# A tuned decay-attention and expert kernel: the old state copied into the sum's bank in eight chunks, and the later chunks' order planned anew

## The chip, the cores and the metric

The kernel runs on one core of a Trainium2 chip. The metric is device microseconds of one execution. A profiled execution gives, beside its time, the span from its first to its last instruction and a trace of every engine.

## The reference

First comes a gated linear attention with a complex decay: for each of 4 batches and 8 heads a 48 x 48 state runs over 768 steps, and its output becomes the rows of a mixture of 8 experts with a fixed capacity. Cut to what matters:

```python
for t in range(S):                       # per batch b and head h
    new_re = ar * S_re - ai * S_im       # ar, ai: a_re, a_im scaled so that the size is at most 0.999
    new_im = ar * S_im + ai * S_re
    S_re, S_im = new_re + k_t v_t^T, new_im
    y[t] = q_t @ S_re
x = y laid out as 3072 tokens of 384 numbers
logits = x @ w_gate                      # 8 experts, each takes 384 tokens, the best pairs first
out[tokens of e] = relu(x[tokens of e] @ w1[e]) @ w2[e]
```

## The kernel before, in words

**Staging.** The 768 steps of a batch are six chunks of 128, so there are 24 chunks, numbered 0 to 23 through all four batches; cc is the chunk's place in its batch. Three chunks make a group (`GROUPS`), eight groups in all. The elementwise work on the decay (square, Ln, Exp, Arctan, Sin on ScalarE, products and running sums on VectorE; stages F1 to F11, S, G1 to G5, A1 to A2, N0, N2, T1 to T3 in `elementwise`) is done per group, and is the bulk of VectorE's and ScalarE's work. T1 and T3 write the sines and cosines `CS`.

**A chunk, stage by stage** (`turns` and `unit`):

- RQ (VectorE): `f <- kq, CS`, the rotation of keys and queries. K (SyncE's DMA queue): six transfers `KQ <- f` stack it for TensorE.
- SC (TensorE): `sc <- KQ`, scores, in two halves. MK (VectorE): `am <- sc, mask`, two halves.
- FL (TensorE): `kp <- ident, KQ`, keys turned, only for cc below 5. KC (ScalarE): `kt <- kp`.
- ST (TensorE): `U <- V, kt`, eight products that are the chunk's part of the state. CA (TensorE): `U <- W, ident`, one product of 384 columns with a unit matrix that adds the old state W to the sum in the same bank. WM (VectorE): `W <- U, KQ`, the sum times the gate is the state for the next chunk. W and its successor lie in two tiles in turn.
- MX (TensorE): `y <- am, V` and `y <- KQ, W`. XC (ScalarE): `xT <- y`. FN (TensorE): `xp <- pick, xT`. XE (ScalarE): `x <- xp`. LR (VectorE): `lg <- xp`, the logits. XS: the store of `x`.
- FI (TensorE): `sc <- mask, f`, products whose result nobody reads, so many for each chunk as the table `FILL` says, three pieces a chunk. They stand ahead of the chunk's scores.

**Two ways to the sum.** Where a chunk is in `SEEDED` (line 691: 20, 21 and 22 before), CA is left out. Instead US (ScalarE, after the WM of the chunk before) copies W into the bank, and ST adds its eight products onto it without a start flag:

```python
U = mine["U"] = sums.pop(i) if i in SEEDED else ps.tile([96, 384], F32, name="U")
...
sums[i + 1] = ps.tile([96, 384], F32, name="U")
nc.scalar.activation(sums[i + 1], W[(cc + 1) % 2][:, :384], AF.Copy)
```

**What sets the order.** `attention` records every step with a cost, its inputs and a number `prio` (the chunk, with a little added or taken off), and then `OFF` adds an offset by the step's kind. `in_order` is a planner: it lets a model of the engines run, and on each engine the ready step with the smallest number goes first. The order it finds is then fixed by dependences (`Queue.follow`), engine by engine, so on the chip each engine works through its list strictly in that order. A step's kind carries ">" where its number is at least `LATE` (99 before, so none does). After the attention the same lists go on with the routing and the experts, which a second planner orders.

Of the kernel before, what the change touches and what calls it, by code (L numbers as in the profile page):

```python
# [21 lines left out]
B, H, S, D = 4, 8, 768, 48  # L22
# [234 lines left out]
def attention(nc, real, tc, z, kq_in, a_re, a_im, v_tok, xd, later):  # L257
# [28 lines left out]
    def op(key, eng, cost, prio, fn, deps=()):  # L286
        kind = key[0][0] if type(key[0]) is tuple else key[0]
        o = Op(eng, cost, fn, [made.get(d) for d in deps], prio)
        o.kind = kind + ("<" if prio < EARLY else ">" if prio >= LATE else "")
        ops.append(o)  # L290
        made[key] = o
        if o.kind.rstrip("<>") in ("lk", "lv"):
            moved(o, 128, (24 if key[0] == "lk" else 12) * T)
        return o
# [161 lines left out]
    def turns(i):  # L456
# [10 lines left out]

        f_free = [("K", i - F_BUFS), ("FI", i - F_BUFS, len(FILL.get(i - F_BUFS, ())) - 1)] if i >= F_BUFS else []
        op(("P0", i), "pool", 0.75, i, lambda: g.tensor_copy(
# [21 lines left out]
    def unit(i):  # L491
# [11 lines left out]
        def keep(n):  # L503
            if ("sc", 0) not in mine:
                mine["sc", 0] = ps.tile([128, 4, 128], F32, name="sc", bufs=2)
            for _ in range(n):
                nc.tensor.matmul(mine["sc", 0].rearrange("p h t -> p (h t)"), tiles["f", i][:, 0, 0, 128:256].bitcast(BF)[:, 1::2],
                                 z.mask.bitcast(BF)[:, None].to_broadcast([128, 2, 256]), start=True, stop=True)
        parts = FILL.get(i, ())
        for n, x in enumerate(parts):  # L510
# [17 lines left out]
        if cc < 5:  # L528
# [14 lines left out]
            def state():  # L543
                U = mine["U"] = sums.pop(i) if i in SEEDED else ps.tile([96, 384], F32, name="U")
                for h in range(8):
                    nc.tensor.matmul(U[:, h * 48:h * 48 + 48], mine["kt"][:, h], v_[:, c * 384 + h * 48:c * 384 + h * 48 + 48],
                                     start=(h == 0 and i not in SEEDED), stop=(h == 7 and (not cc or i in SEEDED)),
                                     skip_group_check=True)
# [4 lines left out]
            op(("ST", i), "pe", 1.33, at - 0.2, state, [("KC", i, 0), ("KC", i, 1), ("lv", gi), ("WM", i - 1), ("WM", i - 2), ("US", i)])  # L553
            if cc and i not in SEEDED:
                op(("CA", i), "pe", 0.65, at - 0.1, carry, [("ST", i), ("WM", i - 1), ("WM", i - 2)])
# [12 lines left out]
            def seed():  # L568
                sums[i + 1] = ps.tile([96, 384], F32, name="U")
                nc.scalar.activation(sums[i + 1], W[(cc + 1) % 2][:, :384], AF.Copy)  # L570
            if i + 1 in SEEDED:
                op(("US", i + 1), "act", 0.371, at + 0.3, seed, [("WM", i)])
# [78 lines left out]
    for o in ops:  # L651
        o.prio += OFF.get(o.kind, 0.0)
    for o in in_order(ops, STEP, HOP, DMA_WAIT, DMA_DONE, START, SLACK):
# [30 lines left out]
DMA_DONE = 1.1  # L684
LATER = [2.4, 4.6, 0.9, 3.6]
START = dict(pe=0.0, act=0.3, dve=2.6, pool=4.3, dma=0.65)
OFF = {"US": 0.0, "A1": 10.399, "A2": -9.822, "BE": 0.131, "CA": -2.118, "F1": -1.107, "F10": 3.443, "F11": 7.184, "F2": -0.925, "F3": 5.421, "F4": 5.223, "F5": -4.22, "F6": 3.011, "F7": -5.852, "F8": -2.715, "F9": -5.359, "FI": 6.816, "FI<": 9.377, "FL": 9.859, "FL<": -5.873, "FN": 12.915, "G1": 1.011, "G2": -1.21, "G3": -11.062, "G4": -0.449, "G5": -6.433, "K": -5.895, "KC": -14.0, "LR": -0.075, "MK": -7.142, "MX": 7.176, "N0": 3.163, "N2": 4.716, "P0": 12.184, "RQ": 2.776, "S": 7.92, "SC": 10.153, "SC<": -1.898, "ST": 11.563, "ST<": -6.332, "T1": 8.558, "T2": 10.974, "T3": -7.584, "TL": -6.667, "WM": -3.298, "XC": -9.548, "XC<": -8.705, "XE": 10.454, "XS": 9.28, "la": -9.643, "la<": -6.574, "later": 0.869, "li": -8.149, "li<": -7.975, "lk": -3.51, "lv": -2.528, "table": -8.414}
CHAIN = ("scalar", "vector", "tensor", "gpsimd", "sync")
F_BUFS, KC_BUFS = 4, 5
FILL = {0: (6, 6, 6), 1: (2, 2, 2), 2: (4, 4, 4), 3: (2, 2, 2), 5: (6, 6, 6), 7: (4, 4, 4), 8: (1, 1, 1), 9: (3, 3, 3), 10: (1, 1, 1), 11: (3, 3, 3), 12: (3, 3, 3), 13: (2, 2, 2)}  # L690
SQ = ()
SEEDED = (20, 21, 22)
EARLY, LATE = 0, 99


class Router:
# [828 lines left out]
```

## Time and profile before

| | us |
|---|---|
| median of 3 runs (lowest to highest) | 488.49 (487.59 to 489.42) |
| the profiled execution, its own time | 489.1 |
| its span, first to last instruction | 487.3 |
| TensorE busy in the span | 430.0 (88%) |
| VectorE busy | 400.8 (82%) |
| ScalarE busy | 309.5 (64%) |

The attention takes the first 222 us of the span and the routing and the experts the rest. The time of an execution is some 2 us more than its span. The tables count an engine as busy while one of its instructions runs; TensorE's ends are modelled.

### The profile page before, as it was taken

Reading aid. Unit: us, or ns where it says so; the run is one execution under the profiler, and the core shown is the slowest. Engines: PE = TensorE matmul, PEld = TensorE weight load, DVE = VectorE, ACT = ScalarE, POOL = GpSimd, SP = SyncE. Lnnn points to the kernel's source line nnn. Section 1 sums busy time; section 2 is a strip of 40 time slices with the busy share of each in tenths; the row PEclk is TensorE's granted clock in tenths of the full one; section 3 lists DMA queues with packets and bytes.
Section 4 is the critical chain, followed back from the end, with each engine's and each line's share of the span. In section 5 each row is a group of like instructions: output and inputs, shape, how many; then the busy total and the mean of one; then the engine's idle time right before and its main releaser. Section 6 shows DMA issues by size and latency. Waiting matters only on the chain.

```text
span 487.3 us, 9823 instructions
## 1 busy us (share of the span) xinstructions
PE 430.0 (88%) x3626; PEld 386.5 (79%) x3626; DVE 400.8 (82%) x1023; ACT 309.5 (64%) x585; POOL 123.6 (25%) x218
## 2 busy tenths in 40 slices
PE   0019999999999999995489899999999999999996
PEld 0006887889789999984378799999989899999995
DVE  6999999999999999845869889998888899434250
ACT  7999988999899849721056448375562837443341
POOL 7321020303031411132031233240503236040202
PEclk9999999999999999996589999999999999999999
DMA  7807886878896855521252526280714438430001
GB/s 259 323 5 205 274 263 201 271 218 271 226 304 196 266 153 160 164 82 67 101 207 98 211 78 228 85 324 18 298 43 179 179 104 342 171 98 0 34 16 50
DMA packets 33104, 82.52 MB, mean 169 GB/s; under 512 B 4352, under 2 KB 23552, under 8 KB 29984
## 3 DMA queue, kind: packets, MB, share of 16 engines
q1 hardware_dynamic: 25632, 41.96, 27.6%
q0 software_dynamic: 6848, 38.95, 21.7%
q10 hardware_dynamic: 576, 0.98, 0.5%
q8 instruction: 29, 0.48, 0.4%
q14 instruction: 19, 0.16, 0.1%
HBM read 53.49 MB, written 9.44 MB: 129 GB/s over the span
## 4 chain that ended last, share of the span: by engine, by line
PE 71%; issue 11%; ACT 7%; DVE 6%; DMA 2%; POOL 1%; SPq 1%; POOLq 1%; ACTq 0%; DVEq 0%
PE acc L136 30%; PE sc L136 14%; PE y L136 8%; PE U L136 7%; PE xp L136 4%; PE kp L136 3%; PE cnt L136 3%; ACT s L136 3%; DVE ind L136 1%; DMA ai<-in_a_im 1%; POOL out L136 1%; ACT L278 1%; PE thr L136 1%; ACT w1h L136 1%; ACT p L136 1%
## 5 line engine op out<-in xcount | busy, mean ns | idle before, releaser
L136 PE MATMUL acc<-w2h,hh 128*128 128x384 f32 x192 | 62.5, 345 | 0.2 <-DVE hl L136 0.2
L136 PE MATMUL acc<-w2h,hl 128*128 128x384 f32 x192 | 62.1, 344 | 0.0
L136 PE MATMUL acc<-w2l,hh 128*128 128x384 f32 x192 | 61.9, 344 | 0.2 <-DVE w2l L136 0.2
L136 PE MATMUL acc<-xl,w1h 128*128 128x384 f32 x192 | 61.2, 343 | 0.1
L136 PE MATMUL acc<-xh,w1l 128*128 128x384 f32 x192 | 61.1, 342 | 0.0
L136 PE MATMUL acc<-xh,w1h 128*128 128x384 f32 x192 | 60.0, 338 | 0.0
L136 PE MATMUL sc<-mask,f 128*128 128x512 bf16 x111 | 28.7, 405 | 35.0 <-DVE f L136 35.0
L136 ACT ACTIVATE hh<-acc 128x384 fp32r<-128x384 f32 x64 | 30.7, 491 | 38.9 <-PE acc L136 37.2
L136 POOL DMA_INDIRECT out<-ot,idx x24 | 25.3, 1055 | 107.7 <-ACT ot L136 102.5
L136 DVE SCALAR_TENSOR_TENSOR hl<-acc,hh 128x384 fp32r<-128x384 f32 x64 | 34.6, 551 | 21.3 <-ACT hh L136 20.6
L136 PEld LDWEIGHTS <-f 128*128 128x128 bf16 x111 | 10.6, 103 | 48.1 <-DVE f L136 35.0
L136 PE MATMUL sc<-KQ 96*128 96x128 f32 x384 | 48.1, 277 | 0.7 <-DMA KQ<-f 0.7
L136 PEld LDWEIGHTS sc<-KQ 96*128 96x128 f32 x384 | 45.1, 192 | 1.5 <-issue 1.4
L136 ACT ACTIVATE parts<-cnt 32x8 f32<-32x8 f32 x120 | 20.2, 168 | 39.9 <-PE cnt L136 37.7
L136 DVE TENSOR_TENSOR f<-kq,CS 128x1536 f32<-128x1536 f32 x24 | 41.6, 1749 | 1.5 <-ACT CS L136 1.0
L136 DVE TENSOR_TENSOR ind<-m,thr 128x768 bf16<-128x768 f32 (+1 forms) x45 | 33.8, 769 | 3.9 <-PE thr L136 2.3
L136 PE MATMUL y<-am,V 128*64 128x128 f32 x384 | 36.5, 278 | 0.0
L136 PEld LDWEIGHTS acc<-w2h,hh 128*128 128x128 f32 x192 | 35.6, 189 | 0.6 <-DVE hl L136 0.6
L136 PEld LDWEIGHTS acc<-w2l,hh 128*128 128x128 f32 x192 | 35.6, 188 | 0.4 <-DVE w2l L136 0.3
L136 POOL DMA_DIRECT2D xd<-x x22 | 13.4, 608 | 88.8 <-ACT x L136 88.5
L136 DVE TENSOR_TENSOR am<-sc,mask 128x512 f32<-128x512 f32 x48 | 31.7, 680 | 5.0 <-PE sc L136 4.8
L136 PEld LDWEIGHTS acc<-w2h,hl 128*128 128x128 f32 x192 | 35.8, 188 | 0.0
(204 smaller groups left out, 1107.9 us busy)
## 6 DMA issues: line engine op xcount, KB each, us to landing
KQ<-f SPq DMA_DIRECT2D x144, 128.5 KB, 2.7
kq<-in_kq SPq DMA_DIRECT2D x8, 1152.0 KB, 7.0
V<-in_v SPq DMA_DIRECT2D x8, 576.0 KB, 5.3
xd<-x POOLq DMA_DIRECT2D x22, 192.0 KB
ar<-in_a_re SPq DMA_DIRECT2D x6, 576.0 KB, 5.1
ai<-in_a_im SPq DMA_DIRECT2D x6, 576.0 KB, 6.2
ar<-in_a_re SPq DMA_DIRECT2D x2, 384.0 KB, 4.2
ar<-in_a_re SPq DMA_DIRECT2D x2, 192.0 KB, 3.9
```

The costliest lines, as they stand in the source:

```text
L136: r = f(*a, **k)
L278: real.scalar.add_instruction(ins)
```

## The change

The three seeded chunks become eight: every chunk of the last two batches that has an old state and a sum (13 to 16 and 19 to 22). For 13, 14, 15, 16 and 19 the copy US is new and the product CA goes. `LATE` is 11.5, so that all steps of the chunks from 12 on get offsets of their own (kinds with ">"), and `FILL` loses its entries for chunks 10 (3 products) and 11 (9) and gains 14 (18) and 18 (12). Of the offsets two stand here for the table.

```diff
-OFF = {"US": 0.0, ..., "F11": 7.184, ...}
+OFF = {..., "F11": 7.184, "F11>": -0.841, ..., "US>": 2.849, ...}
...
-FILL = {0: (6, 6, 6), 1: (2, 2, 2), 2: (4, 4, 4), 3: (2, 2, 2), 5: (6, 6, 6), 7: (4, 4, 4), 8: (1, 1, 1), 9: (3, 3, 3), 10: (1, 1, 1), 11: (3, 3, 3), 12: (3, 3, 3), 13: (2, 2, 2)}
+FILL = {0: (6, 6, 6), 1: (2, 2, 2), 2: (4, 4, 4), 3: (2, 2, 2), 5: (6, 6, 6), 7: (4, 4, 4), 8: (1, 1, 1), 9: (3, 3, 3), 12: (3, 3, 3), 13: (2, 2, 2), 14: (6, 6, 6), 18: (4, 4, 4)}
 SQ = ()
-SEEDED = (20, 21, 22)
-EARLY, LATE = 0, 99
+SEEDED = tuple(range(13, 17)) + tuple(range(19, 23))
+EARLY, LATE = 0, 11.5
```

The order of steps moves on every engine from about 80 us of the span to the attention's end. The routing and the experts keep theirs. Three places follow.

TensorE at the end of the attention, before: `KQ_122` is the stack of chunk 21, `KQ_123` of 22, `KQ_124` of 23. The rows left out are the products `y`.

```order
L136 MATMUL kp<-ident,KQ_122 128x96 x8
L136 MATMUL sc<-KQ_122 128x128 x8
L136 MATMUL U<-V_115,kt 96x48 x8
...
L136 MATMUL kp<-ident,KQ_123 128x96 x8
L136 MATMUL sc<-KQ_123 128x128 x8
L136 MATMUL U<-V_115,kt 96x48 x8
...
L136 MATMUL sc<-KQ_124 128x128 x8
L136 MATMUL xp<-pick,xT 128x112 x8
```

The same stretch in the changed kernel:

```order
L136 MATMUL kp<-ident,KQ_122 128x96 x8
L136 MATMUL sc<-KQ_122 128x128 x8
L136 MATMUL U<-V_113,kt 96x48 x8
L136 MATMUL kp<-ident,KQ_123 128x96 x8
L136 MATMUL sc<-KQ_123 128x128 x8
...
L136 MATMUL U<-V_115,kt 96x48 x8
L136 MATMUL xp<-pick,xT 128x112 x4
...
L136 MATMUL sc<-KQ_124 128x128 x8
L136 MATMUL U<-V_115,kt 96x48 x8
L136 MATMUL xp<-pick,xT 128x112 x4
```

The state products `U` of chunk 20 now stand behind the scores of 21, those of 21 behind the products `y` of chunk 21, and those of 22 behind the scores of 23. The turned outputs `xp` go one by one.

VectorE around the rotation of chunk 21 (`f_118`), before; `ext` is the reduction over the first eighteen chunks' logits.

```order
L136 TENSOR_TENSOR p<-p,s_1615 128x3x128
L136 TENSOR_TENSOR W_109<-U,KQ_125 96x384
L136 SCALAR_TENSOR_TENSOR zi<-zi,s_1624 128x128 x3
L136 TENSOR_TENSOR f_118<-kq,CS 128x6x256
L136 TENSOR_TENSOR am<-sc,mask 128x512 x2
L136 TENSOR_TENSOR f_119<-kq,CS 128x6x256
L136 TENSOR_TENSOR kq<-kq,s_1624 128x3x128
L136 TENSOR_TENSOR kq<-kq,zi 128x3x128
L136 TENSOR_TENSOR W_111<-U,KQ_121 96x384
L136 TENSOR_REDUCE lg_89<-xp 128x16
L136 TENSOR_REDUCE ext<-lg_89 128x2
L136 COPY lg_89<-ext 128x16
```

The same place in the changed kernel:

```order
L136 SCALAR_TENSOR_TENSOR p<-ar,ai 128x3x128
L136 TENSOR_TENSOR am<-sc,mask 128x512
L136 TENSOR_TENSOR p<-p,s_1651 128x3x128
L136 TENSOR_REDUCE lg_89<-xp 128x16
L136 TENSOR_REDUCE ext<-lg_89 128x2
L136 COPY lg_89<-ext 128x16
L136 TENSOR_TENSOR f_118<-kq,CS 128x6x256
L136 TENSOR_TENSOR f_119<-kq,CS 128x6x256
```

One logits reduction, `ext` and its copy have moved ahead of the rotation of chunk 21, and the `W` of chunk 19 (`KQ_125`) has moved behind it. Farther ahead, out of these rows, the step `p <- p, s` (128x3x256) of this group now stands ahead of the rotations of chunks 18 to 20, where it stood behind them.

ScalarE around the sines of chunks 15 to 17 in the changed kernel, where the first of the new copies stands:

```order
L278 ACT_TABLE_LOAD
L136 ACTIVATE xT<-y 128x512
L136 ACTIVATE kt<-kp 128x384 x2
L136 ACTIVATE CS<-neg 128x3x384
L136 ACTIVATE xT<-y 128x512
L136 ACTIVATE U<-W_111 96x384
L136 ACTIVATE x<-xp 128x384 x2
L136 ACTIVATE CS<-p,cb 128x3x384
```

Before, nothing but one `x` stood between the two rows `CS` of this group, and the cosine row came first; the copy `U <- W_111` (for chunk 13) and the outputs of the chunks before are now ahead of the second.

## Rows read from the trace of the kernel before

**Rows 1.** Busy us by stretch: length, PE, PEld, DVE, ACT, POOL; PEclk, DMA share, GB/s.

```profile
127.00:151.00 24.00, 24.00 (x247) 21.07 (x248) 23.40 (x35) 21.52 (x28) 5.27 (x7) 1.00 0.86 264
151.00:175.00 24.00, 24.00 (x277) 21.75 (x275) 23.88 (x40) 19.52 (x27) 6.51 (x8) 1.00 0.67 207
175.00:195.00 20.00, 19.84 (x221) 18.26 (x220) 19.18 (x34) 16.16 (x27) 3.29 (x6) 1.00 0.66 180
...
211.00:223.00 12.00, 10.39 (x121) 9.52 (x120) 3.42 (x10) 3.01 (x6) 2.66 (x14) 1.00 0.27 84
```

**Rows 2.** The chain that ended last, 181 to 220 us: start, us, what.

```profile
181.40 0.66 PE kp L136 x8
...
195.58 0.88 PE xp L136 x8
...
201.71 0.66 PE kp L136 x8
202.37 1.81 PE sc L136 x16
204.19 1.32 PE U L136 x16
...
211.32 2.45 DMA KQ<-f
...
217.93 1.91 PE y L136 x32
```

**Rows 3.** VectorE in order of time, 179 to 208 us: start, us, instruction, idle before.

```profile
179.16 0.95 DVE L136 TENSOR_TENSOR p<-p,s 128x768 f32<-128x768 f32 x1
180.03 0.55 DVE L136 TENSOR_SCALAR neg<-ar 128x384 f32<-128x384 f32 x1
...
193.62 1.76 DVE L136 TENSOR_TENSOR f<-kq,CS 128x1536 f32<-128x1536 f32 x1 [0.43 <-issue]
195.30 1.28 DVE L136 TENSOR_TENSOR am<-sc,mask 128x512 f32<-128x512 f32 x2
...
199.10 0.55 DVE L136 TENSOR_TENSOR W<-U,KQ 96x384 f32<-96x384 f32 x1
200.22 0.23 DVE L136 TENSOR_REDUCE lg<-xp 128x16 f32<-128x64 f32 x1 [0.58 <-ACT x L136]
200.49 0.45 DVE L136 TENSOR_REDUCE ext<-lg 128x2 f32<-128x288 f32 x1
200.97 0.18 DVE L136 COPY lg<-ext 128x16 f32<-128x16 f32 x1
...
206.31 1.76 DVE L136 TENSOR_TENSOR f<-kq,CS 128x1536 f32<-128x1536 f32 x1 [0.53 <-ACT CS L136]
```

**Rows 4.** VectorE at the rotations of chunks 12, 15 and 18, and three scans.

```profile
124.19 3.42 DVE L136 TENSOR_TENSOR f<-kq,CS 128x1536 f32<-128x1536 f32 x2
...
137.38 1.04 DVE L136 TENSOR_TENSOR_SCAN zi<-zi,s 128x128 f32<-128x128 f32 x3
...
148.91 1.75 DVE L136 TENSOR_TENSOR f<-kq,CS 128x1536 f32<-128x1536 f32 x1
...
172.65 1.75 DVE L136 TENSOR_TENSOR f<-kq,CS 128x1536 f32<-128x1536 f32 x1
```

**Rows 5.** The chain earlier: nine filling products, and U with the carry.

```profile
106.81 2.05 PE sc L136 x9
...
189.04 2.01 PE U L136 x18
```

**Rows 6.** TensorE in order of time: the turned keys of chunk 12.

```profile
134.81 0.82 PE L136 MATMUL kp<-ident,KQ 96*128 96x96 f32 x8
```

**Rows 7.** ScalarE in order of time: sines, turned keys, and two of the three copies U.

```profile
147.37 1.16 ACT L136 ACTIVATE CS<-neg 128x1152 f32<-128x1152 int32 x1
148.42 0.87 ACT L136 ACTIVATE kt<-kp 128x384 f32<-128x384 f32 x2
149.16 0.61 ACT L136 ACTIVATE xT<-y 128x512 f32<-128x512 f32 x1
...
193.44 0.47 ACT L136 ACTIVATE U<-W 96x384 f32<-96x384 f32 x1
...
208.56 0.49 ACT L136 ACTIVATE U<-W 96x384 f32<-96x384 f32 x1 [1.98 <-DVE W L136]
```

More of the change, by code (lines that the diff above doesn't have):

```diff
@@ L686 @@
 START = dict(pe=0.0, act=0.3, dve=2.6, pool=4.3, dma=0.65)
-OFF = {"US": 0.0, "A1": 10.399, "A2": -9.822, "BE": 0.131, "CA": -2.118, "F1": -1.107, "F10": 3.443, "F11": 7.184, "F2": -0.925, "F3": 5.421, "F4": 5.223, "F5": -4.22, "F6": 3.011, "F7": -5.852, "F8": -2.715, "F9": -5.359, "FI": 6.816, "FI<": 9.377, "FL": 9.859, "FL<": -5.873, "FN": 12.915, "G1": 1.011, "G2": -1.21, "G3": -11.062, "G4": -0.449, "G5": -6.433, "K": -5.895, "KC": -14.0, "LR": -0.075, "MK": -7.142, "MX": 7.176, "N0": 3.163, "N2": 4.716, "P0": 12.184, "RQ": 2.776, "S": 7.92, "SC": 10.153, "SC<": -1.898, "ST": 11.563, "ST<": -6.332, "T1": 8.558, "T2": 10.974, "T3": -7.584, "TL": -6.667, "WM": -3.298, "XC": -9.548, "XC<": -8.705, "XE": 10.454, "XS": 9.28, "la": -9.643, "la<": -6.574, "later": 0.869, "li": -8.149, "li<": -7.975, "lk": -3.51, "lv": -2.528, "table": -8.414}
+OFF = {"A1": 10.399, "A1>": 12.582, "A2": -9.822, "A2>": -7.131, "BE>": 0.184, "CA": -2.118, "F1": -1.107, "F10": 3.443, "F10>": -2.977, "F11": 7.184, "F11>": -0.841, "F1>": 9.456, "F2": -0.925, "F2>": -4.698, "F3": 5.421, "F3>": 14.0, "F4": 5.223, "F4>": 10.113, "F5": -4.22, "F5>": -2.47, "F6": 3.011, "F6>": -1.065, "F7": -5.852, "F7>": 10.7, "F8": -2.715, "F8>": 0.086, "F9": -5.359, "F9>": 12.455, "FI": 6.816, "FI<": 9.377, "FI>": 4.422, "FL": 9.859, "FL<": -5.873, "FL>": -1.602, "FN": 12.915, "FN>": 6.34, "G1": 1.011, "G1>": -8.004, "G2": -1.21, "G2>": 3.76, "G3": -11.062, "G3>": -4.808, "G4": -0.449, "G4>": 2.176, "G5": -6.433, "G5>": -0.588, "K": -5.895, "K>": 2.748, "KC": -14.0, "KC>": -0.932, "LR": -0.075, "LR>": 5.74, "MK": -7.142, "MK>": -13.968, "MX": 7.176, "MX>": -8.176, "N0": 3.163, "N0>": 1.825, "N2": 4.716, "N2>": 9.631, "P0": 12.184, "P0>": -12.123, "RQ": 2.776, "RQ>": -10.775, "S": 7.92, "S>": 6.55, "SC": 10.153, "SC<": -1.898, "SC>": 0.655, "ST": 11.563, "ST<": -6.332, "ST>": 1.524, "T1": 8.558, "T1>": 2.908, "T2": 10.974, "T2>": -0.665, "T3": -7.584, "T3>": 7.342, "TL": -6.667, "TL>": 4.19, "US>": 2.849, "WM": -3.298, "WM>": 3.698, "XC": -9.548, "XC<": -8.705, "XC>": -5.369, "XE": 10.454, "XE>": -1.616, "XS": 9.28, "XS>": 8.325, "la": -9.643, "la<": -6.574, "la>": 2.746, "later>": -9.256, "li": -8.149, "li<": -7.975, "li>": 3.861, "lk": -3.51, "lk>": 4.282, "lv": -2.528, "lv>": -9.512, "table": -8.414}
```

## The prediction

> **What bounds the kernel now.** I read the busy times by stretch first, then the chain that ended last, then VectorE's and ScalarE's lists in order of time. The change lies in the attention, so only that is costed. In the stretches from 127 to 195 us TensorE is busy all but 0.16 us and VectorE all but 1.5 of 68 us, while ScalarE has 2.5, 4.5 and 3.8 us free [rows 1]. Two engines are full, and the chain shows how they meet: VectorE makes a rotation, the queue stacks it, and TensorE takes it up. The last rotation ends at 206.31 + 1.76 = 208.07 us [rows 3] and its last transfer lands at 211.32 + 2.45 = 213.77 [rows 2], so a stack is there 5.7 us after its rotation. TensorE's last long run begins with the turned keys of chunk 21 at 201.71 and ends with the products y of chunk 23 at 217.93 + 1.91 = 219.84 [rows 2]. The rotation of chunk 21 ends at 195.3 [rows 3], so its stack lands at 201.0, and TensorE comes 0.7 late to it. The attention's end is therefore set by the rotation of chunk 21 plus TensorE's work behind it, as long as TensorE reaches it in time.
>
> **The change part by part.**
>
> Carries: U with the carry takes 2.01 us [rows 5] and without it 1.32 [rows 2], so 0.69 each. Five go: 3.45 us off TensorE.
>
> Fills: nine take 2.05 us [rows 5], 0.228 each. Twelve go at chunks 10 and 11 (2.7), thirty come at 14 and 18 (6.8). TensorE's work as a whole grows by 4.1 - 3.45 = 0.65 us.
>
> Copies: five at 0.48 us [rows 7], 2.4 on ScalarE. Their cover is the free time of ScalarE above. Without it they would delay the sines, and with them the rotations (a rival below).
>
> Moved steps on VectorE, counted from the two orders up to each group's first rotation. Chunk 12: three scans and one logits reduction more, 1.04 + 0.23 [rows 3, 4], some 1.2. Chunk 15: six scans and two reductions more, some 2.4. Chunk 18: p, neg, one mask half and one reduction more, 0.95 + 0.55 + 0.64 + 0.23, less their overlaps, about 2.0 [rows 3]. Chunk 21: a reduction, ext and its copy more, the W of chunk 19 less, 0.23 + 0.45 + 0.18 - 0.55 = 0.3 [rows 3]. So the middle groups' stacks come later and chunk 21's nearly at the old time. The first three are hidden if TensorE is no earlier than the stacks: chunk 12's now lands at 125.9 + 1.2 + 5.7 = 132.8 [rows 4], chunk 18's at 172.65 + 1.75 + 2.0 + 5.7 = 182.1 [rows 4].
>
> Is TensorE in time for chunk 21? It began the turned keys of chunk 12 at 134.81 [rows 6]. Now 2.7 of fills are gone ahead of that, and one xp (0.88 [rows 2]) has come: 133.0, just behind the stack. From there to the keys of chunk 18 it took 181.40 - 134.8 = 46.6 us [rows 2, 6]. Now 6.8 of fills come, four carries (2.8) and one xp (0.9) go: 49.7, so 182.7, behind that stack by 0.6. From the keys of 18 to those of 21 the new order has three kp, three sc, two U, two and a half y and three xp: 2.0 + 5.4 + 2.6 + 4.8 + 2.6 = 17.4 [rows 2], with 0.3 for the seams 17.7, so 200.4.
>
> The stack of chunk 21: VectorE waits 0.43 ahead of that rotation [rows 3], for the cosines. The step p that starts ScalarE's work for them now stands ahead of three rotations (over 5 us), so I let that wait go. 0.3 more work, 0.4 less wait: the stack lands at 200.9, and TensorE begins there with 0.5 in hand.
>
> The last run: the new order has two kp, three sc, three U, three y and two xp up to the end of chunk 23's y, 1.3 + 5.4 + 4.0 + 5.7 + 1.8 = 18.2 [rows 2]. The old one has one U less, 16.9, and took 18.13; the other 1.2 is mostly the wait for chunk 23's stack. That stack comes earlier now, since VectorE's W of chunk 20 stands behind the last rotation (0.55 [rows 3]), and the scores of 23 are asked for only 12.3 us into the run, at 213.2. So that wait goes, and the moved U takes its place: with seams 18.5, end at 219.4. What follows (xp, x, the logits) is as before.
>
> The sum: 219.4 against 219.84, **0.4 us less**. Against the profiled execution's own 489.1 that is 488.7. That execution lies 0.6 above the median of the runs, so against 488.49 I forecast 488.1. The bounds of the unknown part are VectorE's waits: if all 0.8 us that it was free from 175 to 195 [rows 1] goes, 0.4 more is won; if none goes, 0.4 is lost.
>
> **The rivals.**
>
> TensorE comes late (ends slower). The fills taken out at chunks 10 and 11 may be followed by waits of the same size, and then the thirty new ones are pure work. If TensorE still reaches chunk 12 at the old time plus the xp, it comes 2.7 later everywhere, 2.2 of it behind the 0.5 in hand: 488.1 + 2.2 = 490.3. Waits for masks or the W that now stand behind other steps add to that in full; two of 0.5 (the W is 0.55 long [rows 3]) make 491.3. For it: TensorE has no free time in this stretch [rows 1], and the sum grows by 0.65. Against it: by the counts above it is behind the stacks at 12 and 18 by 0.2 and 0.6 only, so real work fills the gap. It decides from 0.5 us of such waits on. Chance 0.23, half of it above 490.9.
>
> ScalarE's queue. A copy that waits for its W holds everything behind it: one copy stood 1.98 us so [rows 7]. Around the sines of chunk 15 the new order has two kt, one xT, two x and one copy more ahead of the second table of sines, 0.87 + 0.6 + 1.0 + 0.5 = 3.0, the x taken like a copy [rows 7], and the old slack is 148.91 - 148.53 = 0.4 [rows 4, 7]. VectorE's own 2.4 covers nearly all. At chunk 21, where 0.3 is the cover, all five copies (2.4) ahead of the sines would cost up to 2.1: 490.2. Against it stand 4.5 and 3.8 us free on ScalarE [rows 1]. Chance 0.12. The Trainium skill (PSUM — Partial Sum Buffer, Engine vs sequencer instructions) states the rule behind this rival: ScalarE's and VectorE's queues are strictly first in, first out. The waiting copy in the rows agrees.
>
> The clock. With gaps where fills stood, the granted clock could fall to 1.2 GHz. It was 1.00 from 211 to 223 us with TensorE busy 10.39 of 12 [rows 1], so gaps of a fraction of a microsecond do nothing. If a stretch with 5 us of work ran at half, 5 us would come on top, 0.5 of it in hand: 492.6. Chance 0.04. The Trainium skill (TensorE: Matmul & The Clock Gate, Part 1) says that the low clock is the default and that only sustained activity lifts it, which speaks against taking fills out; by that rule alone the time would come out at this rival's.
>
> More is won than I see. If chunk 21's rotation came 2.2 us earlier, TensorE being there too, 485.9. VectorE is busy all but 0.8 us in that stretch [rows 1] and has not less to do, which speaks against it. Chance 0.07.
>
> **How the numbers follow.** The forecast has 0.54. Differences within 0.5% (2.4 us, about what a measurement of this kernel can tell from none) run from 486.05 to 490.9. The forecast, ScalarE's rival and half of the late TensorE lie between them, 0.54 + 0.12 + 0.11 = 0.77; for terms that I left out I move 0.07 of that to faster and 0.04 to slower, which leaves 0.66. Slower is the other 0.12 of the late TensorE, the clock's 0.04 and that 0.04: 0.2. Faster is 0.07 + 0.07 = 0.14. The range goes from the forecast with all waits gone (487.7) less the 0.9 by which the runs lie under their median, 486.8, to the late TensorE with its masks, 491.3.
>
> **What would show it.** TensorE's U with unit matrix: 16 instructions, not 26; copies U: 8; fills: 129. The rotation of chunk 21 within 0.5 of 193.5; the keys of 21 at about 200.9, the end of chunk 23's y near 219.4, and no wait for chunk 23's stack. I am wrong if TensorE shows waits over 0.5 us between 105 and 182 or reaches chunk 18 after 183.2, if VectorE waits longer for CS, if the granted clock falls under 1.00 ahead of 220, or if the attention's end moves by over 2.4 us either way.

## The result, and the profile after

The changed kernel takes 493.03 us (median of 6 runs, 490.62 to 498.08) against 487.77 for the kernel before (6 runs, 487.44 to 489.42): a ratio of 1.0108, 95% interval 1.008 to 1.0135. It is 1.1% slower, and the forecast of no difference (488.1, range 486.8 to 491.3) was wrong. A second set of six gave 1.0121 (1.0089 to 1.0153). A ratio leaves out runs that lie over 1.5% above the fastest of their kernel (here the one of 498.08). The changed kernel's runs lie 7.5 us apart, in the second set 4.9, those of the kernel before 2.0.

The profiled run took 493.2 with a span of 491.4. The first two lines below are stretches from the start of rotation 9: to the start of rotation 18, and to the end of the last y. The others are around chunk 13. The columns are those of [rows 1].

```profile
101.27:180.40 79.13, 76.00 (x770) 65.86 (x770) 73.89 (x111) 67.37 (x87) 12.81 (x22) 0.98 0.70 216
101.27:226.70 125.43, 121.40 (x1293) 107.72 (x1291) 108.79 (x173) 96.59 (x137) 21.82 (x40) 0.99 0.64 191
...
140.00:142.00 2.00, 0.54 (x7) 0.57 (x8) 2.00 (x7) 0.70 (x1) 0.00 (x0) 1.00 0.89 220
142.00:144.00 2.00, 2.00 (x9) 0.87 (x8) 1.39 (x3) 1.98 (x4) 0.00 (x0) 0.50 1.03 275
144.00:146.00 2.00, 2.00 (x11) 1.62 (x10) 1.92 (x2) 2.00 (x3) 1.83 (x2) 0.64 0.92 378
```

The same two stretches of the kernel before:

```profile
100.49:172.65 72.16, 72.16 (x748) 62.74 (x748) 71.26 (x106) 65.53 (x82) 16.76 (x21) 1.00 0.77 238
100.49:219.84 119.35, 118.53 (x1285) 106.21 (x1283) 108.74 (x173) 94.14 (x132) 26.70 (x40) 1.00 0.67 202
```

To the last y the new kernel needs 6.1 us more. By TensorE's column that is 2.9 us more busy time and 3.2 more idle; some 1.7 of the busy time are the low clock around chunk 13, since a second profile without it (below) has 119.7 us busy. By VectorE's column, up to rotation 18 it has 2.6 us more work (73.89 - 71.26) and is idle 5.24 us where it was idle 0.90. Of the 5.24 only 1.3 lie ahead of TensorE's wait at chunk 13 (141.46, below) and 4.0 behind it, so this column alone does not tell which engine begins the loss.

VectorE in order of time (start, us, instruction, idle before it and what ended that), with the rotations that answer to [rows 3, 4]:

```profile
112.89 0.69 DVE L136 TENSOR_TENSOR am<-sc,mask 128x512 f32<-128x512 f32 x1 [0.75 <-PE sc L136]
...
127.31 5.07 DVE L136 TENSOR_TENSOR f<-kq,CS 128x1536 f32<-128x1536 f32 x3
...
144.08 1.36 DVE L136 TENSOR_TENSOR kq<-kq,s 128x1152 f32<-128x1152 f32 x1 [0.69 <-ACT s L136]
...
147.92 0.69 DVE L136 TENSOR_TENSOR am<-sc,mask 128x512 f32<-128x512 f32 x1 [1.22 <-PE y L136]
...
150.73 0.23 DVE L136 TENSOR_REDUCE lg<-xp 128x16 f32<-128x64 f32 x1 [1.23 <-PE xp L136]
...
156.17 5.07 DVE L136 TENSOR_TENSOR f<-kq,CS 128x1536 f32<-128x1536 f32 x3
...
180.40 5.09 DVE L136 TENSOR_TENSOR f<-kq,CS 128x1536 f32<-128x1536 f32 x3
...
198.46 3.42 DVE L136 TENSOR_TENSOR f<-kq,CS 128x1536 f32<-128x1536 f32 x2
...
210.26 1.75 DVE L136 TENSOR_TENSOR f<-kq,CS 128x1536 f32<-128x1536 f32 x1
```

Rotation 12 begins 3.1 us later than before (0.8 of it is there before the orders part: the first step in which VectorE's two lists differ begins at 83.64 us, where it began at 82.78), 15 by 7.3, 18 by 7.8, 21 by 4.8, 23 by 4.0. TensorE's keys kp, which answer to [rows 2, 6], and six fills (the second line):

```profile
141.46 1.00 PE L136 MATMUL kp<-ident,KQ 96*128 96x96 f32 x8 [1.89 <-DMA KQ<-f]
142.26 2.76 PE L136 MATMUL sc<-mask,f 128*128 128x512 bf16 x6
...
188.61 0.88 PE L136 MATMUL kp<-ident,KQ 96*128 96x96 f32 x8
...
206.95 0.85 PE L136 MATMUL kp<-ident,KQ 96*128 96x96 f32 x8 [0.18 <-DMA KQ<-f]
...
211.62 0.85 PE L136 MATMUL kp<-ident,KQ 96*128 96x96 f32 x8 [0.69 <-DMA KQ<-f]
```

At chunk 13 TensorE waits 1.89 us for the second stack of its group, and then the granted clock is 0.50 and 0.64: the six fills take 2.76 us (1.46 in the second profile, where the clock is 1.00). Chunk 18 comes at 188.61, 7.2 us later than in [rows 2], and from there to the last y's end (226.70) it is 38.1 us, about as before (219.84 - 181.40 = 38.4).

That second stack is late for two reasons. Rotation 12 begins 2.3 us later than before, counted from rotation 9, and the stack's last transfers are slow. The first line below is from 132.9 to 134.3 us, the other two are from 135.5 to 136.3 (the number of issues, the size of one and the median us from issue to landing; `xd <- x` is the store of x):

```profile
KQ<-f SPq DMA_DIRECT2D x3, 128.5 KB, 2.5
...
xd<-x POOLq DMA_DIRECT2D x2, 192.0 KB, 4.5
KQ<-f SPq DMA_DIRECT2D x2, 128.5 KB, 5.0
```

In the kernel before, one store stood there and the last transfer of chunk 13 took 3.7 us; here it took 5.2, and the 1.5 between them are most of the wait. At chunk 16 the last two took 5.1 and 5.0 us, again with two stores issued meanwhile, and 2.4 and 2.5 before. In the new order x of two chunks is often evicted and stored together. No run moved the stores alone, so their part is seen in the traces and not tested.

Behind the attention this profile is 2.8 us shorter than before (264.7 against 267.5 from the last y to the end of the span). The kernels below show either figure (264.6 to 265.3 us in four profiles, 266.8 to 268.2 in the others), so I don't put it down to the change.

### The profile page after: what moved, and what is told of

The parts are those of the page before. It is cut to its first block, busy times and chain, and to the rows that moved or that the text cites. A ratio compares the mean times of both kernels' runs of the same rounds, so it can differ in the third digit from the quotient of the medians.

```text
span 491.4 us, 9855 instructions
## 1 busy us (share of the span) xinstructions
PE 432.5 (88%) x3634; PEld 387.9 (79%) x3634; DVE 401.0 (82%) x1023; ACT 311.4 (63%) x590; POOL 119.5 (24%) x218
## 4 chain that ended last, share of the span: by engine, by line
PE 63%; issue 12%; ACT 10%; DVE 6%; DMA 4%; SPq 2%; POOL 1%; POOLq 1%; ACTq 0%; DVEq 0%
PE acc L136 30%; PE sc L136 12%; PE y L136 7%; PE U L136 5%; ACT s L136 4%; PE xp L136 3%; PE cnt L136 3%; PE kp L136 2%; SPq L136 2%; DMA KQ<-f 2%; ACT p L136 1%; ACT L278 1%; DMA ai<-in_a_im 1%; DVE ind L136 1%; ACT zi L136 1%
## 5 line engine op out<-in xcount | busy, mean ns | idle before, releaser
L136 PE MATMUL sc<-mask,f 128*128 128x512 bf16 x129 | 34.3, 412 | 35.0 <-DVE f L136 35.0
L136 PEld LDWEIGHTS <-f 128*128 128x128 bf16 x129 | 12.9, 106 | 49.9 <-DVE f L136 35.0
L136 POOL DMA_DIRECT2D xd<-x x22 | 12.1, 550 | 98.8 <-ACT x L136 98.8
L136 PEld LDWEIGHTS acc<-xh,w1l 128*128 128x128 f32 x192 | 35.8, 189 | 0.0
```

The costliest lines, as they stand in the source:

```text
L136: r = f(*a, **k)
```

## The experiments

Ratios are to the kernel before, run beside each on the same chip.

**1. The gap at chunk 13.** The six fills of chunk 13 were put ahead of its first keys, so that TensorE has them to do while it waits.

```diff
+    for k in [('FI', 13, 0), ('FI', 13, 1), ('FI', 13, 2)]:
+        done.remove(made[k])
+        done.insert(done.index(made[('FL', 13, 0)]), made[k])
```

> The changed kernel with one move on TensorE: the six filling multiplies of chunk 13 stand ahead of its first transposes (kp) and no longer behind them. Theory (the gap): in the changed kernel TensorE arrives at kp of chunk 13 at 139.57, waits 1.89 us for the stack that lands at 141.46, and then the granted clock is 0.50 and 0.64 in 142 to 146, so that the six fills take 2.76 us. With the fills in the gap TensorE is busy while it waits: the granted clock stays at 1.00 in 140 to 150, the fills take 1.5 us, scores of 13 begin at about 142.7 and not at 145.0, rotation 15 ends about 2 us earlier than 156.17, and the whole is 1.5 to 2.5 us under the changed kernel (ratio to before 1.006 to 1.008). If the gap is also what makes the changed kernel's times lie 7 us apart, they will lie within 2 us. Rival (work, not clock: VectorE's and ScalarE's order sets rotation 15): the clock may recover, but rotation 15 stays within 0.7 us of 156.2 and the ratio within 0.002 of the changed kernel's 1.0108.

1.0135 (1.009 to 1.018), runs from 493.6 to 501: nothing gained, and neither range held. The clock stays 1.00 at chunk 13, and rotation 15 begins 1.75 us earlier, at 154.42, but the gap turns up at chunk 16 (TensorE's list, then a slice of 4 us):

```profile
168.79 0.85 PE L136 MATMUL kp<-ident,KQ 96*128 96x96 f32 x8 [1.37 <-DMA KQ<-f]
```

```profile
168.00:172.00 4.00, 3.21 (x28) 3.01 (x30) 3.12 (x6) 2.65 (x5) 0.79 (x3) 0.77 0.92 257
```

Next, the twelve fills that chunks 10 and 11 had lost were put back (the others stayed).

```diff
+BACK = {10: (1, 1, 1), 11: (3, 3, 3)}
...
             def scores(hh=hh):
+                if hh == 0:
+                    for x in BACK.get(i, ()):
+                        keep(x)
```

> The changed kernel with the twelve filling multiplies that chunks 10 and 11 had before (3 and 9) put back ahead of their scores; chunks 12, 13, 14 and 18 keep theirs. Theory (the gap): TensorE gets 2.7 us more work between 108 and 125, arrives at kp of chunk 13 at 141 to 142 and no longer waits there for the stack; the granted clock stays at 1.00 in 140 to 150, and the time is 1 to 2.5 us under the changed kernel (1.005 to 1.009). Rival (fills are only work on the path): the 2.7 us are added to the time, 495 to 496.5 us (ratio 1.015 to 1.018), whatever the clock does.

1.0069 (1.0049 to 1.0089). TensorE has 2.7 us more to do and the kernel is 0.4 to 0.5% faster than the changed one. There is no wait at chunk 13, the clock is 1.00, and the six runs lie within 1.4 us. Its lines for chunk 13 and for the stretch to rotation 18:

```profile
140.00:144.00 4.00, 4.00 (x39) 3.38 (x39) 4.00 (x11) 3.65 (x5) 0.00 (x0) 1.00 1.00 239
```

```profile
101.08:178.51 77.43, 76.81 (x784) 66.41 (x784) 73.81 (x111) 67.54 (x87) 14.02 (x22) 1.00 0.71 220
```

So the gap and the clock are one loss, and 0.7% remains without them. What remains is mostly TensorE's own work: to the last y it idles 2.0 us and is busy 122.1, 3.6 more than before, and the thirty late fills (6.8) less five carries (3.45) make 3.4 of that.

**2. Order against copies.** The kernel before with the five copies alone, each right behind its W, and the changed kernel with the carry multiplies instead of the five copies:

```diff
             def carry():
+                if i in MOVED:
+                    return
...
             def decay():
                 v.tensor_tensor(nxt(), ...)
+                if i + 1 in MOVED:
+                    seed()
```

> The kernel before, its order and its fills as they were; only the old state of chunks 13 to 16 and 19 is copied into the sum's bank by ScalarE, right behind each decayed state W, in place of the carry multiply. Five multiplies of 0.69 us leave TensorE, five copies of some 0.48 us come to ScalarE. Theory (the order makes the loss): within 0.5% of before (486.0 to 490.0 us), rotations 15 and 18 within 1 us of 148.91 and 172.65. Rival (the copies make it: each stands in ScalarE's queue and waits for W, and what is behind it is late): slower by 2 to 4 us, with ScalarE's waits for VectorE's W showing it. Second rival (the copies are the useful part): faster by 1 to 3 us.

```diff
             def seed():
+                if i + 1 in MOVED:
+                    return
...
             def state():
...
+                if i in MOVED:
+                    carry()
```

> The changed kernel, its order and its fills, with the copies of chunks 13 to 16 and 19 left out: there TensorE adds the old state by the carry multiply right behind the eight state multiplies. Theory (the order makes the loss): TensorE has 3.45 us more, ScalarE 2.4 us less, and the time is that of the changed kernel, 492 to 494.5 us (ratio 1.008 to 1.014), with rotation 15 at 155 to 157.5. Rival (the copies make it): 487 to 489.5 us, rotation 15 near 149 to 151.

The copies alone cost: 1.0068 (1.0044 to 1.0092), the first rival's range. The order without them is no better: 1.0149 (1.0126 to 1.0172), above either range. In the first of the two TensorE has 2.3 us less to do and idles 4.1 more. ScalarE's list, and what TensorE waits for:

```profile
172.29 0.49 ACT L136 ACTIVATE U<-W 96x384 f32<-96x384 f32 x1 [0.63 <-DVE W L136]
172.72 1.15 ACT L136 ACTIVATE CS<-neg 128x1152 f32<-128x1152 int32 x1
```

```profile
157.95 1.56 PE L136 MATMUL U<-V,kt 128*96 128x48 f32 x16 [1.25 <-ACT U L136]
...
174.40 0.44 PE L136 MATMUL y<-am,V 128*64 128x128 f32 x4 [1.46 <-ACT xT L136]
```

The copy waits for its W, and a sine and an eviction of y stand behind it. That is the rule of the Trainium skill (PSUM — Partial Sum Buffer, Engine vs sequencer instructions) that ScalarE's queue is first in, first out; the rows agree.

**3. The fills.** The changed kernel again; without its 30 late fills; with the old fills; and the last with the carries too, which is the kernel before with the new order alone (the fills of 10 and 11 stand right ahead of those chunks' scores).

```diff
-... lambda x=x: keep(x), ...
+... lambda x=x: keep(x if i not in DROP else 0), ...
...
+DROP = (14, 18)
```

> The changed kernel itself, once more, beside the next three on the same chip. All theories: ratio 1.007 to 1.014. Theory (a gap of TensorE near chunk 13 and the clock that falls after it make its times vary): the runs lie again more than 3 us apart, where those of the kernel before lie within about 2.5; if they lie within 2 us, the spread was not the kernel's.

> The changed kernel, its order and its copies, without the 30 filling multiplies of chunks 14 (18) and 18 (12); those of 12 and 13 stay. Theory (TensorE's time from rotation 9 to the last y is its work and its gaps: 121.4 busy and 4.0 idle in the changed kernel): 6.6 us of work go, but TensorE then arrives earlier at the stacks of 15 to 18 and waits there, so a half to all of it comes back as gaps and as a lower clock: ratio 1.000 to 1.010, with more than 6 us of idle TensorE between rotation 9 and the last y. Rival (the fills are simply work on the path): 5.5 to 6.6 us under the changed kernel, ratio 0.995 to 0.999, idle about 4 us as it was.

> The changed kernel, its order and its copies, with the fills of the kernel before: 12 at chunks 10 and 11, none at 14 and 18. So it differs from the kernel before by the order and the five copies alone. Theory (work and gaps): no gap at chunk 13, gaps at 15 to 18 as in the run without late fills; ratio 1.000 to 1.009. Rival (the order of VectorE is what loses, fills or not): 1.007 to 1.012, as with the fills of 10 and 11 put back. Second rival (fills are simply work): 0.993 to 0.998.

> The same with the carry multiplies of chunks 13 to 16 and 19 in place of the copies: the kernel before with the new order alone. Theory (the order loses, the copies give a part back): 0 to 3.5 us above the run with the old fills and the copies; ratio 1.003 to 1.013. Rival (TensorE idles there anyway, so the carries fill gaps): within 1 us of it. Second rival (the copies are what costs, as in the run with the copies alone, where they cost 0.7%): under it by 1 us or more.

In turn: 1.0121 (1.0089 to 1.0153); 1.0117 (1.0083 to 1.0152) with runs from 490.7 to 505.8; 1.0150 (1.0119 to 1.0181); 1.0120 (1.0086 to 1.0155). The second and the third lie above every range given for them. So the new order alone gives the whole loss, and with the old fills the copies don't help (the intervals of the two overlap, and the profile with the copies has 13 us of low clock, shown at the end). With the order alone TensorE has as many products to the last y as before (x1285); it idles 3.95 us, where it idled 0.82, and is busy 1.1 us longer:

```profile
100.42:224.04 123.62, 119.67 (x1285) 106.66 (x1283) 108.90 (x173) 95.05 (x132) 23.06 (x40) 1.00 0.64 193
```

Without the late fills 30 x 0.228 = 6.8 us of work [rows 5] are gone, TensorE idles 9.2 us to the last y instead of 4.0, and the clock falls three times; two of the slices:

```profile
160.00:164.00 4.00, 1.66 (x16) 1.42 (x18) 3.67 (x6) 3.99 (x7) 0.54 (x1) 0.82 0.75 205
164.00:168.00 4.00, 4.00 (x40) 3.67 (x37) 3.48 (x7) 2.19 (x5) 0.54 (x1) 0.75 0.91 269
```

The second profile of the changed kernel shows it without a fall of the clock (rotation 18, then chunk 13, where its gap was 1.63 us):

```profile
100.82:177.43 76.61, 74.37 (x771) 65.11 (x770) 73.56 (x111) 67.41 (x87) 12.92 (x22) 1.00 0.71 224
...
140.00:144.00 4.00, 3.52 (x28) 2.93 (x29) 3.68 (x7) 2.97 (x5) 0.98 (x1) 1.00 0.90 262
```

That run took 491.57. Over the twelve runs of the changed kernel, the five with a mean granted clock of 0.972 or less took 493.2 to 498.1, the seven with 0.974 or more 490.6 to 492.9. The spread goes with the clock, and some 4 us are lost without it. TensorE's waits in that profile are 1.63, 0.33 and 1.32 us for the second stacks of three groups (chunks 13, 16 and 19; for the last the profile names no releaser, but that stack lands at 191.56 us and its keys begin at 191.96) and 0.25 and 0.56 at 21 and 22; in the first they were 1.89 and 0.68 (13 and 16), 0.18 and 0.69.

**4. What holds the rotations.** VectorE's moved steps were put back behind the rotations in the changed kernel; and, the other way round, the three scan steps were put ahead of rotations 12 and 15 in the kernel before.

The edits write VectorE's whole list out; in short (not the code itself), with RK for the rotation, S for a scan step and LR for a sum of logits:

```python
x = behind(x, [('LR', 7), S(0, 5)], ('RK', 14))
x = behind(x, [('LR', 10), ('LR', 11), S(0, 6), S(1, 6)], ('RK', 17))
x = behind(x, [('LR', 14), ('F11', 7, 0)], ('RK', 20))
```

> The changed kernel with a few of VectorE's steps put back behind the rotations: the first scan of the next group and one sum of logits (lg of chunk 7) behind rotation 14, two scans of the next group and the sums of logits of chunks 10 and 11 behind rotation 17, the logits of chunk 14 and one product (F11 of the last group) behind rotation 20. Nothing else differs; TensorE's list is the same. In the second profile of the changed kernel these take 1.3 us ahead of rotation 12 and 3.5 us more ahead of rotation 15, waits for xp included (0.24; 1.24 and 0.18). Theory (VectorE's order makes the rotations late, and TensorE's idle 4 us come of that): rotation 15 begins at 148.5 to 150 where it began at 153.5, TensorE idles under 2.5 us between rotation 9 and the last y, and the time is 2 to 4 us under the changed kernel, ratio 1.003 to 1.008. Rival (TensorE's own work and order, fills of 14 and 18 among it, set the end): rotation 15 comes as early, but the ratio stays at 1.010 to 1.014.

> The first kernel of this call with the 12 fills of chunks 10 and 11 put back as well. Theory (late rotations and the gap at chunk 13 are two separate losses of the new order): the gap at 13 and the low clock are gone too, the runs lie within 2 us, and the ratio is 0.999 to 1.005, under both the first kernel of this call and the run with the fills put back (1.0069). Rival (TensorE's work sets the end): 1.006 to 1.010.

```python
y = ahead(y, [S(0, 5)], ('RK', 12))
y = ahead(y, [S(0, 6), S(1, 6)], ('RK', 15))
```

> The kernel before with one thing of the new order: on VectorE the first scan of group 5 stands ahead of rotation 12, and the first two scans of group 6 ahead of rotation 15 (each scan step is 0.96 us of three instructions). Theory (VectorE's order makes the loss): rotation 12 0.7 to 1.0 us later, rotation 15 1.5 to 2.9 us later than in the kernel before, and the time 1 to 3 us more, ratio 1.002 to 1.006. Rival (the scans only change places: what is ahead of rotation 12 is not behind it, and TensorE covers the rest): within 0.7 us, ratio 0.9985 to 1.0015.

Both theories missed the first two: 1.0194 (1.0168 to 1.022) and 1.0226 (1.019 to 1.0262). ScalarE's arctangent of the last group needs the product F11 that I moved; it waited 5.09 us, with an eviction of y behind it, and TensorE 3.32 us for that. In the first kernel rotation 15 began at 152.37 and had waited 2.33 us.

In the third the kernel is 1.5% slower (1.0125 to 1.0176), far above both ranges, but the scans are not all that changed. Rotation 12 is 1.3 us later, then the sum of logits of chunk 7 waits 4.28 us, the mask behind it is late, TensorE's fills wait for the mask, and the clock falls:

```profile
133.41 0.23 DVE L136 TENSOR_REDUCE lg<-xp 128x16 f32<-128x64 f32 x1 [4.28 <-ACT x L136]
```

```profile
134.29 3.50 PE L136 MATMUL sc<-mask,f 128*128 128x512 bf16 x9 [2.74 <-DVE am L136]
```

```profile
132.00:136.00 4.00, 1.71 (x6) 0.72 (x6) 2.58 (x4) 1.38 (x2) 0.54 (x1) 0.85 0.81 229
136.00:140.00 4.00, 4.00 (x25) 2.69 (x24) 3.97 (x6) 0.00 (x0) 0.00 (x0) 0.72 0.70 191
```

In the kernel before, that sum waited for TensorE's xp alone and ran 4.8 us ahead of ScalarE's x of the same chunk (VectorE, then ScalarE):

```profile
127.52 0.21 DVE L136 TENSOR_REDUCE lg<-xp 128x16 f32<-128x64 f32 x1
```

```profile
132.28 0.47 ACT L136 ACTIVATE x<-xp 128x384 f32<-128x384 f32 x1
```

Both read xp. With the new list the sum is issued behind that x (now at 132.91 us) and its instruction also waits for ScalarE's semaphore, which it did not before. So the run turned a dependence around as well, and it does not show what the scans cost by themselves.

Then VectorE's steps put back as in the first kernel, without the last group's part and with the fills of 10 and 11 back; ScalarE's second sine of group 5 moved up to the first; and both.

```diff
+lists["act"].remove(made["T3", 5, 0])
+lists["act"].insert(lists["act"].index(made["T1", 5, 0]) + 1, made["T3", 5, 0])
```

> The changed kernel with the fills of chunks 10 and 11 put back, and VectorE's steps (three scans of three, the sums of logits of chunks 7, 10 and 11) behind rotations 14 and 17; the last group's order is untouched. Theory (joint): VectorE is ready for rotation 15 at 152.2, waits some 2.4 us for the second sine, rotation 15 stays at 154 to 155, ratio within 0.002 of 1.0069. Rival (VectorE alone holds it, and the sines come earlier with it): rotation 15 at 152 to 153, ratio 1.002 to 1.005. The run with the last group's product moved as well (1.0226) does not speak against either: there ScalarE's arctangent of the last group waited for that product.

> The changed kernel with the 12 fills of chunks 10 and 11 put back (as in the run of that name, 1.0069, rotation 15 at 154.61), and in ScalarE's queue the second sine of group 5 right behind the first, ahead of an eviction of y, the copy for chunk 14 and two evictions of xp that stand between them (1.65 us). Theory (VectorE and ScalarE hold rotation 15 jointly: VectorE is ready at 154.6, the sines at 154.5): rotation 15 stays within 0.5 us of 154.6, and the ratio within 0.002 of 1.0069. Rival (ScalarE alone holds it): rotation 15 at 152.6 to 153.4, ratio 1.003 to 1.005.

> Both edits of the two runs beside it. Theory (joint): only now rotation 15 comes earlier, at 152.2 to 153.2 (1.4 to 2.4 us before 154.6), rotation 18 and the last y by 1 to 2.4 us, ratio 1.002 to 1.005. Rival (what is moved is paid for behind the rotations, on VectorE, or by xT and kt, which TensorE waits for): rotation 15 early, the last y not, ratio 1.006 or more.

1.0105 (1.008 to 1.0129), 1.0078 (1.0051 to 1.0104) and 1.0070 (1.0043 to 1.0097); rotation 15 at 154.41, 154.45 and 152.29. (The copy between the two sines is the first of the eight, for chunk 13, and not for 14 as expected above.) With VectorE's steps back, VectorE is ready at 152.0 and waits for the second sine (ScalarE, then VectorE):

```profile
150.29 1.18 ACT L136 ACTIVATE CS<-neg 128x1152 f32<-128x1152 int32 x1
151.42 0.60 ACT L136 ACTIVATE xT<-y 128x512 f32<-128x512 f32 x1
151.91 0.48 ACT L136 ACTIVATE U<-W 96x384 f32<-96x384 f32 x1
152.33 0.85 ACT L136 ACTIVATE x<-xp 128x384 f32<-128x384 f32 x2
153.07 1.25 ACT L136 ACTIVATE CS<-p,cb 128x1152 f32<-128x1152 f32 x1
```

```profile
154.41 1.76 DVE L136 TENSOR_TENSOR f<-kq,CS 128x1536 f32<-128x1536 f32 x1 [2.41 <-issue]
```

So with these fills VectorE and ScalarE hold rotation 15 jointly, as the theory said: only both edits move it. But that gains nothing, as the rival said: from rotation 9 to 18 it is 77.37 us with both edits and 77.43 without, the last y comes 0.9 us earlier against rotation 9, and the ratio is the same. The reason stands in the same rows, in TensorE's column. The first line goes to rotation 18, the second to the first keys of chunk 18, and the third is that stretch in the kernel before:

```profile
100.67:178.04 77.37, 77.10 (x792) 66.75 (x792) 73.54 (x111) 67.98 (x87) 14.48 (x22) 1.00 0.70 221
100.67:185.74 85.07, 84.80 (x873) 72.68 (x871) 81.24 (x120) 73.87 (x96) 16.09 (x25) 1.00 0.69 216
...
100.49:181.23 80.74, 80.74 (x850) 70.58 (x849) 79.82 (x117) 68.03 (x87) 18.38 (x24) 1.00 0.75 230
```

TensorE is busy all but 0.27 us, while VectorE is idle 3.8 of 77.37 and waits mostly for TensorE's outputs. To chunk 18 TensorE has 4.1 us more to do, as the thirty late fills (6.8) less four carries (2.8) give. With both edits the order's waits up to chunk 18 are gone, then, and what is left is the late fills' own time. Both edits without the late fills were not run, so it stays open whether that kernel would equal the one before.

**5. In search of a version that beats both.** Copies in the old order, each behind a step of ScalarE that others wait for: for 13, 15 and 16; and for 19 alone.

```diff
+    behind = {13: ("XC", 12), 15: ("KC", 15, 1), 16: ("XC", 15)}
...
         o.fn()
+        if o in [made[x] for x in behind.values()]:
+            later_.pop(0)()
```

> The kernel before with copies for chunks 13, 15 and 16 alone (14 and 19 keep the carry), and each copy in ScalarE's queue behind a step that a rotation or TensorE waits for, and not ahead of it: for 13 behind both sines of group 5 and the eviction of y, for 15 behind the second kt, for 16 behind both sines of group 6 and the eviction of y. 3 x 0.69 = 2.1 us leave TensorE. Theory (in the run with the copies alone the place in ScalarE's queue cost, not the copy): 0.5 to 2 us faster than before, ratio 0.996 to 0.999. Rival (a copy makes a chain U, W, copy, U that TensorE waits for wherever it stands, and what it saves turns into idle time): ratio 1.000 to 1.006. No rival gives less than 0.995, since VectorE is 99% busy there too.

> The kernel before with the copy for chunk 19 alone, in ScalarE's queue behind the eviction of y of chunk 18: one multiply of 0.69 us leaves TensorE's last stretch (kp of chunk 18 to the last y, 38.6 us, 99% busy). Theory (that stretch is TensorE's own, everything ahead of it is the rotations'): the stretch is 37.7 to 38.3, and the time 0 to 0.8 us less, ratio 0.998 to 1.000. Rival (the copy's place among ScalarE's steps delays the last group, as where all five were copied): 1.001 to 1.005.

0.9988 (0.9973 to 1.0004), not told from no change, and 1.0020 (1.0002 to 1.0038), 0.2% slower and barely clear of it. With the places mended the three copies cost nothing. The run with all five had copies for 14 and 19 as well, so its loss may lie in the places or in those two; no run separates that. Nor do the carries taken off TensorE gain: it is busy 1.1 us less to the last y and idles 2.4 us more. For chunk 19 the last stretch became 39.8 us, not shorter: TensorE waited 1.3 us for an eviction on ScalarE, and the mean clock was 0.77 and 0.80 in the two slices from 196 to 204. No kernel here beats the one before beyond doubt.

## Why the prediction was wrong

**The step that failed is the one on the middle groups**: "The first three are hidden if TensorE is no earlier than the stacks", with the moved steps costed by their own length (1.2, 2.4 and 2.0 us) and the waits of VectorE and TensorE there put at nothing. VectorE's work was sized nearly right: up to rotation 18 VectorE has 2.3 to 2.6 us more. But it also idles 3.05 us in one profile of the changed kernel and 5.24 in the other, where it idled 0.90. In the first profile the waits are for TensorE's scores, xp and y, and for an exponential of ScalarE. Rotation 18 so comes 4.45 or 6.97 us later against rotation 9, not 2.0. The run with the order alone has the same account (77.31 us from rotation 9 to 18, 73.71 of it busy). [Rows 1] showed VectorE full, so I took a moved step for a shift by its length; the traces show that the engines then wait for one another in turn. Which of these waits is the first cause is read from the traces and not shown by a run.

TensorE's path, in the terms of the forecast's sum:

| TensorE, us | forecast | first profile | second profile |
|---|---|---|---|
| first keys of chunk 12 at | 133.0 | 135.62 | 134.89 |
| from there to those of 18 | 49.7 | 52.99 | 50.71 |
| to those of 21 | 18.2 | 18.34 | 19.70 |
| to the last y's end | 18.5 | 19.75 | 19.62 |
| the end | 219.4 | 226.70 | 224.92 |

The first row was misread: for the 2.7 us of fills that go, two xp come ahead of chunk 12 and not one (43 instructions xp since rotation 9 against 27, eight a chunk), so TensorE is no earlier there (34.35 us after rotation 9, before 34.32). In the second row the waits at chunks 13 and 16 are 2.57 and 1.96 us; without them the second profile has 48.8, under the forecast.

**Only each group's first stack was checked.** Whether TensorE is in time was worked out for chunks 12, 18 and 21. The second stack of a group lands later: that of 13 at 141.3, 12.3 us after rotation 12 ended (before 10.8), and TensorE was there at 139.57. This is the check whose lack cost most: 2.57 of the 4.03 us that TensorE idles to the last y are at the second stacks of 13 and 16, and 3.28 of 4.37 in the second profile at those of 13, 16 and 19. The run with the fills of 10 and 11 put back shows that the gap at 13, with the clock, is about 0.4% and the spread.

**The clock** was a rival with a chance of 0.04. It fell in many of the runs that left TensorE gaps. The sign against it ("gaps of a fraction of a microsecond do nothing") did not hold in every run: in the changed kernel the gap was 1.89 us, but with the old fills the clock fell behind two gaps of 0.99 and 0.62. The rule cited for it (the Trainium skill, TensorE: Matmul & The Clock Gate, Part 1: only sustained activity lifts the clock) pointed the right way, and the rows agree as far as that. That the rival's 492.6 us is near the time measured is luck in part, since more than half of the loss stays where the clock is 1.00. **TensorE late** (0.23) was the nearest rival: its sign, waits over 0.5 us between 105 and 182, came true, and in the first profile so did its condition, TensorE at chunk 12 at the old time plus one xp (135.7). But its price, the late fills as pure work, is not what the changed kernel paid, since TensorE then waits for stacks and taking those fills out gained nothing; it is what is left where the waits are gone (fills back, both edits). **ScalarE's queue** (0.12) was seen in the run with the copies alone, and at rotation 15 once VectorE's steps were put back; in the changed kernel itself VectorE does not wait there for the sines.

**Behind chunk 18** the sum forecast 219.4 - 182.7 = 36.7 us. It was 38.1 and 39.3 in the two profiles, and 37.4 to 39.8 in all the other kernels but one (42.3, with the clock low twice). The wait for chunk 23's stack was 0.66 us before and not most of 1.2; the rest was work that the prices left out (17.5 us busy, priced at 16.9):

```profile
214.13 2.02 PE L136 MATMUL sc<-KQ 96*128 96x128 f32 x16 [0.66 <-DMA KQ<-f]
```

"So that wait goes" was half right: it went, and waits at 21 and 22 came (0.18 and 0.69), as the y of chunk 21 now stands behind the scores of 22. Since this stretch stays within some 2.5 us whatever stands ahead of it, TensorE's arrival at chunk 18 sets most of the end, and not rotation 21, as I had put it.

**What held**: the counts and the prices of carries, copies and fills, and chunk 23's stack in time. The two lines of the tile U (durations in ns: shortest, median, longest) show 16 instructions with the unit matrix, two for each of eight carries, and 8 copies, and the page shows 129 fills:

```profile
L136 PE MATMUL U<-W,ident x16: 486/508/529, 52.8 to 131.6; 96*96 96x384 f32 x16
L136 ACT ACTIVATE U<-W x8: 483/488/503, 153.6 to 218.4; 96x384 f32<-96x384 f32 x8
```

```profile
L136 PE MATMUL sc<-mask,f 128*128 128x512 bf16 x129 | 34.3, 412 | 35.0 <-DVE f L136 35.0
```

**Open**: which of the moved steps begins the first waits, between rotations 9 and 12 (2.3 us, of which 1.2 is work); how much of the waits at the second stacks is the rotations and how much the paired stores; and whether both edits without the late fills would lose anything. Moving the last group's steps back with ScalarE's list was not tried.

## What to carry to other kernels

Where two engines are full and a third is nearly so, a step moved ahead of a shared point costs its length only if nobody waits on the way: count, on every engine, what then stands behind the late piece, and check every item of a group and not the first, with the other transfers that run beside its own. Fills are not free time to be taken out: before one is removed, ask what TensorE finds when it gets there earlier. They are not free to put in either: once TensorE no longer waits, they are its path, so read the full engine's column again after every edit. Work taken off the busiest engine gains nothing where another engine's list sets the next meeting point. And when one list is rewritten to test an order, compare what each instruction waits for before and after, since a dependence can turn around.

## What was not expected of the hardware

The length of a gap does not decide alone whether the granted clock falls: it fell after idle times of 1.89 us (changed kernel, chunk 13), 1.37 (chunk 16, first experiment) and 1.26 (copy for 19 alone), and did not after 1.63 (changed kernel, second profile), 1.25 and 1.46 (the run with the copies alone). In the run with the old fills no gap there was over 1 us, and the clock was at its lower level for 13 us behind two of them:

```profile
160.01 0.44 PE L136 MATMUL y<-am,V 128*64 128x128 f32 x4 [0.99 <-DVE am L136]
161.07 0.44 PE L136 MATMUL y<-KQ,W 96*64 96x128 f32 x4 [0.62 <-DVE W L136]
```

```profile
162.00:175.00 13.00, 13.00 (x82) 12.44 (x80) 9.08 (x17) 7.10 (x12) 1.50 (x6) 0.50 0.76 219
```

With the order alone the same two gaps were 0.28 and 0.62 us, and it stayed at 1.00. What TensorE did before differed, and no run here separates that. The figures between 0.50 and 1.00 are means: in slices of half a microsecond the clock of the changed kernel is 0.50 to 0.52 from 142.0 to 145.0, 0.57 in the next and 1.00 from 145.5 on.

The six transfers of a stack take 2.3 to 2.5 us each from issue to landing for chunk 12 of the changed kernel, where no other transfer is issued meanwhile; the last two of chunk 13 take 4.8 and 5.2, with two stores of x issued among them.
